# Pooled attention with a mixture-of-depths block on one core: two pairs of batches in block products, two key buffers, gate weights spread by TensorE, another order

## The chip, the cores and the metric

The kernel runs on one core of a Trainium2 chip. The core has five engines that work side by side, each through a queue of its own that it takes strictly in order: TensorE (PE, matrix products; the loading of its weights is shown as PEld), VectorE (DVE), ScalarE (ACT), GpSimd (POOL) and SyncE (SP, which here only issues transfers). The metric is the device time of one execution in microseconds (us), the median of several runs.

## What is computed

Eight batches (8 heads, 576 positions, head size 64) go through an attention whose keys and values are first averaged over eight neighbouring positions. The output, as rows of 512 numbers, goes through a mixture-of-depths block: in each batch the 128 rows with the highest gate score get a two-layer network added, the other rows stay as they are.

```python
k_p = k.reshape(B, H, Sp, pool, D).mean(axis=3)          # pool = 8
v_p = v.reshape(B, H, Sp, pool, D).mean(axis=3)
...
attn = attn / (np.sum(attn, axis=-1, keepdims=True) + 1e-09)
return np.matmul(attn, v_p).astype(np.float32)
...
scores = np.einsum('bsd,d->bs', x, w_gate)
out = x.copy()
for b in range(B):
    top_idx = np.argpartition(-scores[b], capacity)[:capacity]
    xe = x[b, top_idx]
    h = np.maximum(xe @ w1, 0.0)
    ye = h @ w2
    g = 1.0 / (1.0 + np.exp(-scores[b, top_idx]))
    out[b, top_idx] = x[b, top_idx] + g[:, None] * ye
```

The first layer is 512 by 1024, the second 1024 by 512.

## The kernel before

The work is cut into some 770 small steps, each with a name, an engine (or two or three engines that could do it), the buffers that it reads and writes, and a bank of PSUM. Three tables of numbers fix the program: `ORDER` lists all steps in one order, from which each engine takes its own steps as its queue; `HOMES` says which PSUM bank a group of products uses; `TURNS` says which of its engines a step runs on. Steps of different engines wait for each other only through the data.

For each batch b the steps are, with the names that the prediction uses:

- loads of keys, queries and values (k, q, v) from SP, 1 to 1.2 MB each. There is one key buffer `KR`, and two each of `QR` and `VR`.
- pooling of the keys and values in three halvings (kp, va on DVE or POOL; for batch 0 as products on PE), a product with the gate weights (vg, vt), copies (vd on ACT, then vl on POOL) that give the pooled values their last form; transposes of keys and queries (kh, kt, qt).
- scores on PE (s at line 635, sl at 652), exponentials on ACT (x, xl; lines 619 and 622), products with the values on PE (a at line 724, al at 736), reciprocals and scaling (r, z, n), and the store of the rows (o) from SP or ACT into the output.
- gate scores (sc), ranking by comparison of every row with every other (c where the row is spread by PE, cs where it goes through memory; line 825), a one-hot matrix (oh), its product with the position numbers on PE (pk, line 848), the reduction to an index (tk), and then on POOL the index (ix, line 858) with the gather of the 128 chosen rows from the output (line 859). PE turns the gathered rows (tu, line 879), DVE computes their gate (gd, line 866).
- the two layers: `dense(b)` has 8 products up (u, line 903; 8 records of the trace each) and 8 down (d, line 917). POOL scatters the result (pt, line 932).

Batches 6 and 7 are done together by `twin(6, 7)`: both layers as two-by-two block products in the manner of Strassen and Winograd, seven block products in place of eight (p1 to p7, line 999, 16 records each; q1 to q7, line 1063, 8 records each). For this the sums of weight blocks (wt, wr), of row blocks (sa) and of hidden blocks (sd) are formed by DVE and POOL at line 963 (`sum_`), and the products' outputs are put together by DVE (line 1012, `add_bank`) and ACT. The weight sums live in the buffers `QR` and `VR`, so they follow the last query and value. The list of products in one `twin` depends on DVE and ACT between them:

```python
        product(j7, 1.79, up(T[2][0], s3[0], j7, False), [T[2][1], s3[1]], p + 4, "p7")
        r, ws = claim(kr, m3[1])
        add_bank(m3[0], ws, j7, m1[0], [m1[1]] + r, p - 5000, "mb")
        product(j5, 1.79, up(T[0][0], s1[0], j5, False), [T[0][1], s1[1]], p + 5, "p5")
```

The transfers of SP and ACT share eight lanes, taken in turn; a transfer does not start before the one that held its lane eight transfers earlier has landed, and while it waits, the queue of its engine stands still.

Of the kernel before, what the change touches and what calls it, by code (L numbers as in the profile page):

```python
# [96 lines left out]
"""  # L97
TABLE = [[int(x) for x in t.split()] for t in (ORDER, HOMES, TURNS)]
ON_PE = (0,)
AGO = 500  # L100
BY_ROW = (4,5,6,7)
ON_CHIP = ()
PAIRED = ((6,7),)


class Plan:

# [1409 lines left out]
```

## Time and profile before

| | |
|---|---|
| median of the runs | 234.33 us (234.19 to 234.65) |
| the profiled execution | 235.51 us, of which the traced span is 233.7 us |
| PE busy | 210.5 us, 90% of the span |
| DVE, POOL, ACT busy | 152.3, 119.0 and 77.4 us |
| mean granted TensorE clock | 0.973 of full speed |
| bytes moved | 48.37 MB, a mean of 207 GB/s |

The span is the time between the first and the last event of the trace; 1.81 us of the profiled execution lie around it. PE is busy nearly all of the second half; its gaps lie in the first half, where the transfers are dense as well. The rows themselves stand in a section further down.

### The profile page before, as it was taken

Reading aid. Unit: us, or ns where it says so; the run is one execution under the profiler, and the core shown is the slowest. Engines: PE = TensorE matmul, PEld = TensorE weight load, DVE = VectorE, ACT = ScalarE, POOL = GpSimd, SP = SyncE. Lnnn points to the kernel's source line nnn. Section 1 sums busy time; section 2 is a strip of 40 time slices with the busy share of each in tenths; the row PEclk is TensorE's granted clock in tenths of the full one; section 3 lists DMA queues with packets and bytes.
Section 4 is the critical chain, followed back from the end, with each engine's and each line's share of the span. In section 5 each row is a group of like instructions: output and inputs, shape, how many; then the busy total and the mean of one; then the engine's idle time right before and its main releaser. Section 6 shows DMA issues by size and latency. Waiting matters only on the chain. (4 is left out here: it accounts for less than half of the span.)

```text
span 233.7 us, 6973 instructions
## 1 busy us (share of the span) xinstructions
PE 210.5 (90%) x2886; PEld 144.4 (62%) x2886; DVE 152.3 (65%) x362; ACT 77.4 (33%) x269; POOL 119.0 (51%) x155
## 2 busy tenths in 40 slices
PE   7869799757788999997899999999999999999990
PEld 3464444524535898743454799736488965986880
DVE  4268799944797996887429499973995511128460
ACT  2006356617563024524326243313460340010100
POOL 7016797968995499528031054144600556870531
PEclk9999999995899999999799999999999999999997
DMA  6999989999999489989921622434206441000112
GB/s 190 349 403 337 385 276 340 307 382 383 383 400 405 173 234 382 391 291 326 414 67 24 195 66 72 144 113 76 70 0 185 147 127 46 3 1 0 50 45 97
DMA packets 17815, 48.37 MB, mean 207 GB/s; under 512 B 2416, under 2 KB 2544, under 8 KB 15984
## 3 DMA queue, kind: packets, MB, share of 16 engines
q1 hardware_dynamic: 13552, 39.04, 46.8%
q10 hardware_dynamic: 2944, 4.62, 6.5%
q0 software_dynamic: 1280, 4.20, 5.5%
q8 instruction: 24, 0.39, 0.7%
q14 instruction: 15, 0.12, 0.2%
HBM read 36.31 MB, written 11.54 MB: 205 GB/s over the span
## 5 line engine op out<-in xcount | busy, mean ns | idle before, releaser
L903 PE MATMUL pJ<-xg,w 128*128 128x128 f32 x256 | 31.3, 279 | 0.0
L903 PEld LDWEIGHTS pJ<-xg,w 128*128 128x128 f32 x256 | 29.4, 192 | 2.9 <-issue 2.5
L932 POOL DMA_INDIRECT out_dram<-y,ix x8 | 8.9, 1118 | 42.0 <-DVE y L922 37.1
L917 PE MATMUL pA<-w,ht 128*128 128x512 f32 x48 | 24.0, 630 | 0.0
L619 ACT ACTIVATE em<-pG 128x1024 f32<-128x1024 f32 x16 | 16.4, 1028 | 22.3 <-PE pG L635 18.1
L917 PE MATMUL pJ<-w,ht 128*128 128x512 f32 x48 | 23.5, 606 | 0.0
L613 DVE STREAM_TRANSPOSE qt<-qr 128x1280 f32<-128x1280 f32 (+1 forms) x16 | 21.5, 1351 | 0.9 <-DMA qr<-in_q_dram 0.9
L635 PE MATMUL pG<-qt,kt 32*64 32x256 f32 (+1 forms) x512 | 19.6, 413 | 2.1 <-ACT em L619 1.2
L825 DVE SCALAR_TENSOR_TENSOR cmp<-row,sc,lar 128x576 bf16<-128x576 f32 (+1 forms) x20 | 17.5, 877 | 3.6 <-DMA row<-score_line 3.3
L682 POOL TENSOR_TENSOR vr<-vr 128x512 f32<-128x512 f32 (+1 forms) x12 | 19.4, 1618 | 0.0
L635 PEld LDWEIGHTS pG<-qt,kt 32*64 32x64 f32 x512 | 10.0, 133 | 12.1 <-ACT em L619 3.7
L585 POOL TENSOR_TENSOR kr<-kr 128x512 f32<-128x512 f32 (+1 forms) x8 | 11.3, 1410 | 11.4 <-DMA kr<-in_k_dram 11.4
L736 PE MATMUL pG<-vl,el 32*64 32x264 f32 x156 | 13.6, 425 | 3.4 <-POOL vl L707 2.8
L776 ACT ACTIVATE xs<-pG,rz 128x64 f32<-128x64 f32 (+1 forms) x64 | 14.0, 336 | 5.8 <-DVE rz L767 4.5
L724 PE MATMUL pG<-vs,em 64*64 64x66 f32 x624 | 14.7, 224 | 1.2 <-issue 0.9
L866 DVE SCALAR_TENSOR_TENSOR dots<-xr,wr 128x512 bf16<-128x512 f32 x8 | 8.7, 1083 | 10.7 <-DMA xr<-out_dram,ix 10.7
L724 PEld LDWEIGHTS pG<-vs,em 64*64 64x64 f32 x624 | 12.5, 135 | 4.4 <-issue 2.4
L858 POOL TENSOR_SCALAR ix<-tk 128x1 int32<-128x1 f32 x8 | 2.2, 273 | 25.4 <-DVE tk L854 22.5
L917 PEld LDWEIGHTS pA<-w,ht 128*128 128x128 f32 x48 | 8.8, 202 | 9.1 <-issue 9.1
L917 PEld LDWEIGHTS pJ<-w,ht 128*128 128x128 f32 x48 | 8.2, 190 | 7.4 <-issue 7.4
L859 POOL DMA_INDIRECT xr<-out_dram,ix x8 | 9.0, 1119 | 6.2 <-DMA out_dram<-xs 3.1
L903 PEld LDWEIGHTS pG<-xg,w 128*128 128x128 f32 x96 | 11.4, 192 | 1.0 <-issue 1.0
(210 smaller groups left out, 425.9 us busy)
## 6 DMA issues: line engine op xcount, KB each, us to landing
vr<-in_v_dram SPq DMA_DIRECT2D x8, 1024.0 KB, 8.0
kr<-in_k_dram SPq DMA_DIRECT2D x7, 1152.0 KB, 7.8
qr<-in_q_dram SPq DMA_DIRECT2D x7, 1152.0 KB, 6.4
out_dram<-xs SPq DMA_DIRECT2D x18, 256.0 KB, 8.2
w<-in_moe_w_dram SPq DMA_DIRECT2D x4, 1024.0 KB, 8.1
out_dram<-xs ACTq DMA_DIRECT2D x14, 256.0 KB, 4.9
vr<-in_v_dram SPq DMA_DIRECT2D x16, 64.0 KB
out_dram<-xs SPq DMA_DIRECT2D x7, 128.0 KB
```

Source lines behind the costliest of these rows:

```text
L585: e.tensor_tensor(out=x[:, a:z, 0:2], in0=x[:, a:z, 0:2], in1=x[:, a:z, 2:4], op=OP.add)
L613: nc.vector.transpose(out=QT[b % 2].rearrange("p j x t g -> p t (j x) g")[:, lo:hi], in_=QR[b % 2][:, lo:hi].rearrange("p t (x g) -> p t x ...
L619: note(nc.scalar.activation(to[:, :, 0:256].rearrange("p m (h x) -> p m h x", h=2), of[:, :, :, 0:16].rearrange("p m h t g -> p m h (t g)" ...
L635: note(nc.tensor.matmul(pG[64 * s : 64 * s + 64, r, 0:n], KT[i][rows, j, (SP - NL) * s + NL : (SP - NL) * s + SP], QT[i][rows, j, 2 * s : ...
L682: g.tensor_tensor(out=x[:, a:z, 0:4], in0=x[:, a:z, 0:4], in1=x[:, a:z, 4:8], op=OP.add)
L724: note(nc.tensor.matmul(acc[64 * z : 64 * z + 64, s, E * m : E * m + E], EM[h][i][64 * s : 64 * s + 64, m, AT[c] + 64 * z : AT[c] + 64 * z ...
L736: note(nc.tensor.matmul(pair(jobs[c])[64 * z : 64 * z + 64, s, 0 : NP * E], EL[i][x : x + 32, AT[c] + 64 * z : AT[c] + 64 * z + 64], VL[i] ...
L776: note(nc.scalar.activation(to[:, s, m], o[:, s, m, 0:D], AF.Copy, scale=rz[:, NP * s + m : NP * s + m + 1]))
L825: note(nc.vector.scalar_tensor_tensor(cmp[0:n], row()[0:n, 0:S], SC[i][0:n, c : c + 1], after_, op0=OP.subtract, op1=OP.is_ge, accum_out=R ...
L859: j = nc.gpsimd.indirect_dma_start(out=XR[x], out_offset=None, in_=out_rows[0 : (b + 1) * S], in_offset=bass.IndirectOffsetOnAxis(ap=IX[x] ...
L903: note(nc.tensor.matmul(single(ju)[:, cap * f : cap * f + cap], w1[g][:, d, 128 * f : 128 * f + 128], XG[i][:, d, :], start=(d == 0), stop ...
L917: note(nc.tensor.matmul(single(jd)[0:cap, :], HT[i][f // 4][:, f % 4, :], w2[f // 4][:, f % 4, :], start=(f == 0), stop=(f == FB - 1)))
```

## The change

- `PAIRED` holds two pairs: batches 4 and 5 are done by a `twin` as well, so four batches are left to `dense`. The weight sums are formed once, for the first pair.
- `KR` is two buffers, even and odd batches apart. The results of the second layer in `twin` (N tiles) sit in `KR[1]` and no longer behind the M tiles in the one buffer.
- The gate weights came as two broadcasts of 112 KB and one of 256 KB from memory. Now 2 KB are loaded, two products with a row of ones spread them on PE (gw0, gw1), and two copies store them (gc0, gc1).
- The gate score (sc) and the one-hot matrix (oh) may also run on POOL: sc of batches 0, 1 and 3 to 7, and oh of batches 2, 3 and 5 do. Other steps changed engine in the table too (DVE has 257 steps before and 261 now, POOL 83 and 99, ACT 120 and 131, SP 79 and 71, PE 231 and 215).
- Some helper tiles are in bf16; the test that the ranks are sound counts now the found rows (`found`) and not the sum of the ranks.
- All three tables are new.

```diff
 ORDER = """
-    0 2 16 4 763 12 11 759 25 23 17 18 760 5 14 24 15 6 26 3 20 38 22 21 27 7 33 13 40 28 89 30 99 29 41 31 39 42 43
+    2 16 15 4 18 17 0 20 768 3 6 11 12 769 26 7 19 27 92 28 767 23 5 29 30 31 102 101 25 32 771 41 42 24 14 43 36 13
...
-PAIRED = ((6,7),)
+SHARED = 0
+PAIRED = ((4, 5), (6, 7))
...
-    KR = sb("kr", [128, TG, D])
+    KR = sb("kr", [128, TG, D], n=2)
...
-            dma(KR, src, 128 * 256 * TG, p, (), [("KR", 0), ("KR", 1)], name=f"k{b}")
+            dma(KR[b % 2], src, 128 * 256 * TG, p, (), [("KR", b % 2, 0), ("KR", b % 2, 1)], name=f"k{b}")
...
-        for x in range(2):
-            dma(WG[64 * x : 64 * x + 64].rearrange("p m e -> p (m e)")[:, 0 : DM - D], bass.AP(tensor=t, offset=o + D * x, ap=[[0, 64], [1, DM - D]]),
-                64 * 1792, 2.4, (), [("WG", x)], rate=330e3, cost=0.5, free=True, name=f"g{x}")
+        add("POOL", 0.12, lambda: nc.gpsimd.memset(onerow, 1.0), (), ["onerow"], -90, name="onerow")
+        dma(WR[0:1], bass.AP(tensor=t, offset=o, ap=[[0, 1], [1, DM]]), 2048, -80, (), ["WR"], rate=2e3, cost=0.5, free=True, name="g0")
...
+        def wide():
+            note(nc.tensor.matmul(single(jb)[:, 0:DM], onerow, WR[0:1], start=True, stop=True))
...
-        dma(WR, bass.AP(tensor=t, offset=o, ap=[[0, 128], [1, DM]]), 128 * 2048, 150, (), ["WR"], rate=350e3, cost=0.5, free=True, name="w3")
...
-        def score():
-            nc.vector.tensor_tensor(out=SS[i], in0=ZA[:, b, :, :, 1], in1=RZ[i], op=OP.mult)
-            nc.vector.tensor_reduce(out=SC[i], in_=SS[i], axis=AX.X, op=OP.add)
...
+        def score(e):
+            engine(e).tensor_tensor(out=SS[i], in0=ZA[:, b, :, :, 1], in1=RZ[i], op=OP.mult)
+            if e == "DVE":
+                nc.vector.tensor_reduce(out=SC[i], in_=SS[i], axis=AX.X, op=OP.add)
+                return
+            for w in (4, 2):
+                nc.gpsimd.tensor_tensor(out=SS[i][:, :, 0:w], in0=SS[i][:, :, 0:w], in1=SS[i][:, :, w : 2 * w], op=OP.add)
+            nc.gpsimd.tensor_tensor(out=SC[i], in0=SS[i][:, :, 0], in1=SS[i][:, :, 1], op=OP.add)
...
-        both((("DVE", 1.1), ("ACT", 2.45)), True, one_hot, [("RK", b, c) for c in range(NC)] + ["slots", "ones"], [held, "apart"], p + 0.6, name=f"oh{b}")
+                    engine(e).tensor_scalar(OH[:, c, :], mine(c), RK[:, b, c], None, op0=OP.is_equal)
+        both((("DVE", 1.2), ("ACT", 2.7), ("POOL", 2.1)), True, one_hot, [("RK", b, c) for c in range(NC)] + ["slots", "ones"], ["OH", "apart"], p + 0.6, name=f"oh{b}")
...
-        m1, m3 = (part(KR, f"M{t}", kr, 512 * t, 512, 4) for t in range(2))
+        m1, m3 = (part(KR[0], f"M{t}", kr, 512 * t, 512, 4) for t in range(2))
...
-        n1, n3, v3q, v2q, v2p = (part(KR, f"N{t}", kr, 1024 + 256 * t, 256, 1) for t in range(5))
+        n1, n3, v3q, v2q, v2p = (part(KR[1], f"N{t}", ks, 256 * t, 256, 1) for t in range(5))
```

What the new tables do is seen in the queues. Three places follow; a name with a number is one buffer; the line numbers of these steps are 16 higher in the changed kernel (25 for the turning of gathered rows).

The first is ACT's queue where batch 0's ranking ends and the pooled values of batch 2 are copied (`vs0`, the step vd2), in the kernel before:

```order
L837 ACTIVATE apart_115<-slots_152,rk_112 128x128 x5
L838 ACTIVATE oh_114<-apart_115,ones_154 128x640
L760 ACTIVATE za_146<-pG_166,eps_147 128x8
L761 COPY za_146<-pG_166 128x8
L435 DMA out_0_dram<-xs03_95 16x8x512
L701 COPY vs0_87<-vs0_87 32x66 x2
L760 ACTIVATE za_146<-pA_167,eps_147 128x8
```

And the same place in the changed kernel:

```order
L436 DMA out_0_dram<-xs00_94 16x8x512
L436 DMA out_0_dram<-xs04_98 16x4x512
L776 ACTIVATE za_146<-pG_165,eps_147 128x8
L777 COPY za_146<-pG_165 128x8
L865 ACTIVATE apart_116<-slots_152,rk_113 128x128 x5
L866 ACTIVATE oh_115<-apart_116,ones_154 128x640
L717 COPY vs0_88<-vs0_88 32x66 x2
```

Before, the store of `xs03` (o03) stood right ahead of the copy; now two other stores (o00 and o04) stand ahead of it, with the one-hot matrix between.

The second is PE's queue up to the turning of batch 2's gathered rows (`xr2`, tu2, last row). Before, it ended so:

```order
L917 MATMUL pA_167<-w20_144,ht00_136 128x512
L724 MATMUL pJ_168<-vs1_88,em01_82 64x66 x16
L724 MATMUL pG_166<-vs1_88,em11_84 64x66 x16
L736 MATMUL pJ_168<-vl1_90,el1_86 64x264
L736 MATMUL pG_166<-vl1_90,el1_86 64x264
L736 MATMUL pJ_168<-vl1_90,el1_86 64x264
L736 MATMUL pG_166<-vl1_90,el1_86 64x264
L736 MATMUL pJ_168<-vl1_90,el1_86 64x264
L736 MATMUL pG_166<-vl1_90,el1_86 64x264
L736 MATMUL pJ_168<-vl1_90,el1_86 64x264
L736 MATMUL pG_166<-vl1_90,el1_86 64x264
L879 MATMUL pG_166<-ident_151,xr2_132 128x128 x4
```

In the changed kernel it ends so:

```order
L933 MATMUL pJ_167<-w20_144,ht00_136 128x512
L933 MATMUL pJ_167<-w21_145,ht01_137 128x512 x3
L740 MATMUL pG_165<-vs0_88,em00_82 64x66 x16
L740 MATMUL pG_165<-vs0_88,em10_84 64x66 x16
L752 MATMUL pG_165<-vl0_90,el0_86 64x264 x8
L933 MATMUL pJ_167<-w21_145,ht01_137 128x512
L933 MATMUL pJ_167<-w20_144,ht10_138 128x512 x2
L838 MATMUL pA_166<-ident_151,sc1_109 128x128 x4
L838 MATMUL pA_166<-ident_151,sc1_109 128x64
L904 MATMUL pG_165<-ident_151,xr2_132 128x128 x4
```

Between batch 2's pick (pk2) and this turning stood six d products, two blocks of scores, one block of value products and the spreading of a score row (sp). Now ten d products, the value products of more than a whole block (72 at line 740 and 18 at 752, of which the rows show 32 and 8) and an sp stand there.

The third is the end of PE's queue. Before, the last rows of the program were these (batches 6 and 7):

```order
L1063 MATMUL pA_167<-w20_144,ht00_136 128x256 x4
L1063 MATMUL pG_166<-vr0_70,qt1_80 128x256 x4
L1063 MATMUL pG_166<-vr1_71,qt1_80 128x256 x4
L1063 MATMUL pG_166<-vr0_70,qt1_80 128x256 x4
L1063 MATMUL pA_167<-w21_145,ht01_137 128x256 x4
L1063 MATMUL pG_166<-vr1_71,ht11_139 128x256 x4
L1063 MATMUL pG_166<-w21_145,qt1_80 128x256 x4
```

In the changed kernel they are these (line 1015 is the first layer of a pair, 1079 the second, 1142 the sum for the final test):

```order
L1079 MATMUL pA_166<-w21_145,qt1_81 128x256 x4
L1015 MATMUL pG_165<-qt0_80,qr0_69 128x128 x8
L1142 MATMUL pJ_167<-seen_159,ones_154 1x2
L1015 MATMUL pG_165<-xg1_135,qr1_70 128x128 x8
L1079 MATMUL pG_165<-w20_144,ht00_136 128x256 x4
L1015 MATMUL pG_165<-qt0_80,w11_143 128x128 x8
L1079 MATMUL pA_166<-vr1_72,qt1_81 128x256 x4
L1079 MATMUL pA_166<-vr0_71,qt1_81 128x256 x4
L1079 MATMUL pG_165<-vr0_71,qt1_81 128x256 x4
L1079 MATMUL pG_165<-w21_145,ht01_137 128x256 x4
L1079 MATMUL pG_165<-w21_145,qt1_81 128x256 x4
L1079 MATMUL pA_166<-vr1_72,ht11_139 128x256 x4
```

Before, products of `dense` batches stood among the pair's first-layer products (line 917 rows, not shown); now the second pair's products have only the end of the first pair's among them.

## Rows read from the trace of the kernel before

**Rows 1.** The page, part 1: busy time, share of the span, instructions.
```profile
PE 210.5 (90%) x2886; PEld 144.4 (62%) x2886; DVE 152.3 (65%) x362; ACT 77.4 (33%) x269; POOL 119.0 (51%) x155
```

**Rows 2.** Stretches: length, busy PE, PEld, DVE, ACT, POOL, granted clock, DMA share, GB/s.
```profile
0.00:75.34 75.34, 60.67 (x1123) 35.09 (x1123) 54.16 (x118) 33.43 (x114) 51.85 (x83) 0.95 0.97 349
53.70:60.50 6.80, 6.32 (x124) 4.10 (x132) 4.26 (x10) 3.69 (x19) 6.27 (x10) 0.50 1.03 374
75.34:227.75 152.41, 149.78 (x1767) 109.27 (x1763) 97.66 (x243) 44.01 (x155) 66.02 (x70) 0.99 0.43 141
99.20:109.74 10.54, 10.54 (x167) 5.14 (x166) 8.26 (x17) 3.18 (x7) 5.36 (x6) 1.00 0.89 303
111.70:115.20 3.50, 3.40 (x7) 1.91 (x8) 2.08 (x5) 1.36 (x2) 0.00 (x0) 0.51 1.08 435
180.00:228.00 48.00, 47.74 (x287) 38.02 (x285) 19.70 (x51) 6.87 (x16) 24.76 (x24) 1.00 0.16 51
```

**Rows 3.** The chain that ended last: start, time on the chain, what.
```profile
183.54 2.68 PE pJ L903 x24
186.22 3.44 PE pA L917 x8
...
198.54 5.36 PE pG L999 x48
...
217.38 5.18 PE pG L1063 x24
...
227.78 0.50 DVE y L1069
```

**Rows 4.** PE's waits: for what, us in total, times, the longest.
```profile
PE pG L736 <- POOL vl L707: 2.8, 1, 2.8
...
PE pG L879 <- DMA xr<-out_dram,ix: 2.1, 1, 2.1
...
PE pA L724 <- DVE cmp L825: 1.5, 1, 1.5
PE pJ L1109 <- DVE tk L854: 1.2, 1, 1.2
PE pG L635 <- ACT em L619: 1.2, 1, 1.2
...
PE pG L635 <- ACT za L761: 0.8, 1, 0.8
```

**Rows 5.** Timeline of ACT, 44 to 58 us: start, length, what, idle before.
```profile
47.46 0.16 ACT L761 COPY za<-pG 128x8 f32<-128x8 f32 x1
52.25 0.56 ACTq L435 DMA_DIRECT2D out_dram<-xs  x1
52.85 0.51 ACT L701 COPY vs<-vs 32x66 f32<-32x66 f32 x2 [5.23 <-DMA vr<-in_v_dram]
```

**Rows 6.** Timeline of SP's transfers, 41 to 47 us.
```profile
41.54 2.63 SPq L435 DMA_DIRECT2D vr<-in_v_dram  x2
```

**Rows 7.** Timeline of POOL, 47 to 56 us.
```profile
53.45 0.62 POOL L707 TENSOR_TENSOR vl<-vs,inside 128x264 f32<-128x264 f32 x1 [1.62 <-ACT vs L701]
```

**Rows 8.** Timeline of PE, 46 to 64 us: the first product after the stop.
```profile
54.12 0.69 PE L736 MATMUL pG<-vl,el 32*64 32x264 f32 x1 [2.80 <-POOL vl L707]
```

**Rows 9.** Timeline of PE, 98.8 to 116.5 us, around batch 2's gather.
```profile
99.13 0.28 PE L848 MATMUL pA<-aux,oh 128*128 128x2 bf16 x5
...
107.94 0.70 PE L724 MATMUL pJ<-vs,em 64*64 64x66 f32 x32
...
111.80 1.11 PE L879 MATMUL pG<-ident,xr 128*128 128x128 f32 x4 [2.06 <-DMA xr<-out_dram,ix]
```

**Rows 10.** Timeline of DVE, 158 to 168 us: the gate product of batch 4.
```profile
162.11 3.07 DVE L866 SCALAR_TENSOR_TENSOR dots<-xr,wr 128x512 bf16<-128x512 f32 x1
```

**Rows 11.** Timeline of POOL, the same stretch: a weight sum.
```profile
162.26 2.36 POOL L963 TENSOR_TENSOR qr<-w,w 128x1024 f32<-128x1024 f32 x1
```

**Rows 12.** The tile `dots`, all eight gate products: shortest, median, longest, ns.
```profile
L866 DVE SCALAR_TENSOR_TENSOR dots<-xr,wr x8: 674/692/3072, 70.7 to 214.2; 128x512 bf16<-128x512 f32 x8
```

More of the change, by code (lines that the diff above doesn't have):

```diff
@@ L340, in direct_path @@
     VL = sb("vl", [128, NP, E], n=2)
[L341 removed]
+    WG = sb("wg", [128, NP + 1, D])
+    onerow = sb("onerow", [1, 128])
     XS = [[sb(f"xs{i}{c}", [128, DM]) for c in range(NC)] for i in range(2)]
@@ L398, in single @@
         return pG[:, x] if x < 4 else (pA, pJ)[x // 2 - 2][:, x % 2]
-    beside = {}
+    beside, turns = {}, {}
     def note(ins, other=None):
@@ L478, in line @@
             nc.gpsimd.memset(RK, -1.0)
-        add("POOL", 3.1, line, (), ["slots"] + [(x, i, c) for x in ("SS", "RZ") for i in range(2) for c in range(NC)]
+        add("POOL", 3.3, line, (), ["slots"] + [(x, i, c) for x in ("SS", "RZ") for i in range(2) for c in range(NC)]
             + [("RK", b, c) for b in range(B) for c in range(NC)] + [("VR", i, 1) for i in range(2)], -89, name="line")
@@ L524, in small @@
             nc.gpsimd.memset(want[:, 0:1], float(128 * B * NC * H))
-            nc.gpsimd.memset(want[:, 1:2], float(B * (S * (S - 1) // 2 - 64)))
-        add("POOL", 0.6, small, (), ["ones", "want"] + [("Z", b, NC - 1) for b in range(B)], -60, name="small")
+            nc.gpsimd.memset(want[:, 1:2], float(B * cap))
+            nc.gpsimd.memset(seen, 0.0)
+        add("POOL", 0.6, small, (), ["ones", "want", "seen0", "seen1"] + [("Z", b, NC - 1) for b in range(B)], -60, name="small")
     def load_kq(b):
@@ L556, in load_gate, with halves @@
         t, o = moe_w_gate.tensor, moe_w_gate.offset
-        for x in range(2):
-            dma(WG[64 * x : 64 * x + 64].rearrange("p m e -> p (m e)")[:, 0 : DM - D], bass.AP(tensor=t, offset=o + D * x, ap=[[0, 64], [1, DM - D]]),
-                64 * 1792, 2.4, (), [("WG", x)], rate=330e3, cost=0.5, free=True, name=f"g{x}")
+        add("POOL", 0.12, lambda: nc.gpsimd.memset(onerow, 1.0), (), ["onerow"], -90, name="onerow")
+        dma(WR[0:1], bass.AP(tensor=t, offset=o, ap=[[0, 1], [1, DM]]), 2048, -80, (), ["WR"], rate=2e3, cost=0.5, free=True, name="g0")
+        ja, jb = plan.job(ONES), plan.job(ONES)
+        def halves():
+            for x in range(2):
+                note(nc.tensor.matmul(single(ja)[64 * x : 64 * x + 64, 0 : NP * D], onerow[:, 0:64],
+                                 WR[0:1].rearrange("p (m x d) -> p m x d", x=2, d=D)[:, :, x], start=True, stop=True))
+        def wide():
+            note(nc.tensor.matmul(single(jb)[:, 0:DM], onerow, WR[0:1], start=True, stop=True))
+        add("PE", 0.6, halves, ["onerow", "WR"], [], 10, job=ja, mode=12864, name="gw0")
+        add("PE", 0.86, wide, ["onerow", "WR"], [], 11, job=jb, name="gw1")
+        both((("DVE", 0.4), ("ACT", 0.4)), False, lambda e: copy(e, WG[:, 0:NP], single(ja)[:, 0 : NP * D].rearrange("p (m d) -> p m d", d=D)),
+             [], [("WG", 0)], 10, job=ja, name="gc0")
+        both((("DVE", 0.65), ("ACT", 0.62)), False, lambda e: copy(e, WR, single(jb)[:, 0:DM]), [], ["WR"], 11, job=jb, name="gc1")
         for x in range(2):
@@ L586, in go @@
                 e.tensor_tensor(out=KS[:, a:z], in0=x[:, a:z, 0], in1=x[:, a:z, 1], op=OP.add)
-            both((("DVE", (1.35, 1.15)[n]), ("POOL", (2.41, 2.14)[n])), b < 2, go, [("KR", n)], [("KR", n), ("KS", n)], 100 * b - 60 + n,
+            both((("DVE", (1.35, 1.15)[n]), ("POOL", (2.41, 2.14)[n])), b < 2, go, [("KR", b % 2, n)], [("KR", b % 2, n), ("KS", n)], 100 * b - 60 + n,
                  name=f"kp{b}{n}")
@@ L689, in gate @@
             engine(e).tensor_tensor(out=x[:, :, 2], in0=VS[i][:, :, 0:D], in1=WG[:, :, 0:D], op=OP.mult)
-        both((("DVE", 0.5), ("POOL", 0.88)), b < 1, gate, [("VS", i, 0), ("VS", i, 1), ("WG", 0), ("WG", 1), ("WGL", 0), ("WGL", 1)], [("VR", i, 0), ("VR", i, 1)], p, name=f"vg{b}")
+        both((("DVE", 0.5), ("POOL", 0.88)), b < 1, gate, [("VS", i, 0), ("VS", i, 1), ("WG", 0), ("WGL", 0), ("WGL", 1)], [("VR", i, 0), ("VR", i, 1)], p, name=f"vg{b}")
         def total():
@@ L794, in rank @@
         p = 100 * b + 20
-        def score():
-            nc.vector.tensor_tensor(out=SS[i], in0=ZA[:, b, :, :, 1], in1=RZ[i], op=OP.mult)
-            nc.vector.tensor_reduce(out=SC[i], in_=SS[i], axis=AX.X, op=OP.add)
-        add("DVE", 0.52, score, [("RZ", i, c) for c in range(NC)], [("SC", i)] + [("SS", i, c) for c in range(NC)], p - 70,
+        def score(e):
[6 more added lines that the diff above has]
+            nc.gpsimd.tensor_tensor(out=SC[i], in0=SS[i][:, :, 0], in1=SS[i][:, :, 1], op=OP.add)
+        both((("DVE", 0.7), ("POOL", 0.9)), True, score, [("RZ", i, c) for c in range(NC)], [("SC", i)] + [("SS", i, c) for c in range(NC)], p - 70,
             name=f"sc{b}")
@@ L821, in rank, with count, mine @@
             n = ROWS[c]
-            def count(c=c, n=n):
+            def count(e, c=c, n=n):
+                row_ = row()[0:n, 0:S]
+                to = (cmpa if c < SHARED else cmp)[0:n]
+                turns[b, c] = e
+                if e == "ACT":
+                    note(nc.scalar.activation(to, row_, AF.Sign, bias=SC[i][0:n, c : c + 1], scale=-1.0, accum_out=RK[0:n, b, c]))
+                    return
                 after_ = LAT[0:n, LAST - OFF[c] : LAST - OFF[c] + S] if jr is not None else LAR[0:n, NC - 1 - c : NC - 1 - c + S]
-                note(nc.vector.scalar_tensor_tensor(cmp[0:n], row()[0:n, 0:S], SC[i][0:n, c : c + 1], after_,
+                note(nc.vector.scalar_tensor_tensor(to, row_, SC[i][0:n, c : c + 1], after_,
                                                     op0=OP.subtract, op1=OP.is_ge, accum_out=RK[0:n, b, c]))
-            if jr is None:
-                add("DVE", 0.9, count, ["ROW", ("SC", i), "LAR"], [("RK", b, c), "cmp"], p + c * 0.1, name=f"cs{b}{c}")
-            else:
-                add("DVE", 0.87, count, [("SC", i), "LAT"], [("RK", b, c), "cmp"], p + c * 0.1, job=jr, name=f"c{b}{c}")
-        one, held = (OH, "OH") if b not in ON_CHIP else (apart, "apart")
+            alts = (("DVE", 0.88), ("ACT", 0.95))[: 1 + (c < SHARED)]
+            key = "cmpa" if c < SHARED else "cmp"
+            both(alts, True, count, (["ROW", "LAR"] if jr is None else ["LAT"]) + [("SC", i)], [("RK", b, c), key], p + c * 0.1,
+                 job=jr, name=f"cs{b}{c}" if jr is None else f"c{b}{c}")
+        def mine(c):
+            return slots if turns[b, c] == "DVE" else odd
         def one_hot(e):
@@ L862, in index @@
             gath[b] = [j]
[L863 removed]
+        add("POOL", 1.9, index, [("TK", b)] + [("ROWS", b, c) for c in range(NC)], [("IX", x), ("XR", x)], p - 90,
             late=2.4, mark=b, name=f"ix{b}")
[L866 to L867 removed]
+        add("DVE", 1.0, lambda: nc.vector.scalar_tensor_tensor(cmp[0:cap, 0:DM], XR[x], 1.0, WR[0:cap], op0=OP.mult, op1=OP.mult, accum_out=GV[x]),
+            [("XR", x), "WR"], [("GV", x), "cmp"], p, name=f"gd{b}")
         add("ACT", 0.25, lambda: nc.scalar.activation(GV[x], GV[x], AF.Exp, scale=-1.0), (), [("GV", x)], p, name=f"ge{b}")
@@ L949, in twin @@
         vr = [[("VR", i, h) for h in range(2)] for i in range(2)]
-        kr = [("KR", 0), ("KR", 1)]
+        kr, ks = ([("KR", i, n) for n in range(2)] for i in range(2))
         qt = [[("QT", i, h) for h in range(2)] for i in range(2)]
```

80 lines of the change are left out of this document (33 added, 47 removed), and 86 rows, old and new, of tables (HOMES, ORDER, TURNS).

## The prediction, made before the changed kernel had run

> **What bounds the kernel now.** I read the page's busy times first: PE works 90% of the span, no other engine over 65% [rows 1]. So the second view was the stretches. From the first product of `dense(0)` at 75.34 to the last product at 227.75 PE is busy 149.78 of 152.41 us; in the 75.34 us before that only 60.67, with the transfers at 0.97 of their time and 349 GB/s [rows 2]. PE is the bound behind 75, and what feeds it is the bound ahead of it. The third view was the granted clock: two stretches, 53.70 to 60.50 and 111.70 to 115.20, ran at 0.50 and 0.51 [rows 2], the lower level of 1.2 GHz; half their length, 3.4 and 1.7 us, is lost work even though PE counts as busy. Each stands behind a wait of PE: 2.80 us at 54.12 for the pooled values [rows 8] and 2.06 at 111.80 for gathered rows [rows 9]. The fourth view, PE's waits, names these two as the longest that a new order can move, and four smaller ones of 1.5, 1.2, 1.2 and 0.8 [rows 4]. Behind the last product only its blend of 0.50 at 227.78 [rows 3], a scatter and the end of the span remain; both kernels end so.
>
> The sum is made against the profiled execution's own 235.5; the median of the runs is 1.2 lower, and the forecast is given on the median.
>
> **The products.** By the chain, 24 records of u take 2.68 us and 8 of d 3.44 [rows 3]. A u has 8 records, so 0.893; a d has 2, so 0.86. Two dense batches are 16 of each: 14.3 + 13.8 = 28.05. Forty-eight records of p take 5.36 and 24 of q 5.18: 1.787 per p (16 records), 1.727 per q (8). Seven of each are 24.6. **-3.5**. The pair brings no weight sums of its own, but some two dozen more additions, copies and scalings on DVE, ACT and POOL. They lie beside PE: from 180 to 228 DVE was busy 19.70 of 48 us and POOL 24.76 [rows 2]. Where they don't, they are a cost of the handovers, below.
>
> **The stop at 50 to 60.** ACT finished a copy at 47.6 and then stood until 52.25, when the store o03 left; the copy vd2 behind it began at 52.85 [rows 5], vl at 53.45 [rows 7], PE's products at 54.12 [rows 8]. o03 waited for its lane, held by the values of batch 3 that SP issued at 41.54 [rows 6]. The new queue has o00 and o04 there. Their lanes are held by the last piece of batch 2's own values, for which vd2 needs to wait anyway, and by batch 3's queries, which SP issues two transfers later. So I take the whole stop as gone: 2.80 of wait and 3.4 of clock, **-6.2** (bounds 0 and -6.2). Late next are batch 0's comparisons and the one-hot on ACT, ahead of vd2 in the new queue.
>
> **The gather of batch 2.** Its pick began at 99.13 and its rows were there at 111.80, 12.7 us later; PE had 10.5 of work until 109.74 [rows 2, 9]. The new queue holds ten d (8.6) and the value products: 64 records at line 724 with 16 at 736 took 1.80 from 107.94 [rows 9] to 109.74, and 144 and 36 stand there now, 4.05. With 12.7 of work even without the sp, the wait is covered, if barely: 2.06 and 1.7 of clock, **-3.8** (bounds 0 and -3.8).
>
> **Early waits.** Batch 1's keys have a buffer of their own and stand third in SP's queue, and 0.48 MB of broadcasts (1.4 us at 349 GB/s) are gone from the saturated stretch. The four smaller waits sum to 4.7 [rows 4]. Some are ranking that only moves; I take half, **-2.3** (bounds 0 and -4.7). The products and copies that spread the gate weights run before the first keys have landed; without that cover they cost about 1, two copies of the size of the 0.69 of a gate product [rows 12].
>
> **What comes back.** Three things are new on PE's path. Batches 0 and 1 have their gathers earlier, where transfers are dense: one wait like that of batch 2 with its clock, 3.8. The second pair stands at the end without dense products between its block products, so each must find its sums ready. And 16 more steps run on POOL: while a weight sum of 2.36 ran there [rows 11], a gate product took 3.07 on DVE in place of the median's 0.69 [rows 10, 12], a loss of 2.4. I take one such meeting on the path: **+6.2** (bounds 0 and +12.4, both twice).
>
> The Trainium skill, page "SBUF — State Buffer", section "Who interferes with whom", says that a VectorE instruction with two SBUF inputs and a GpSimd instruction that reads SBUF exclude each other for the whole instruction, whichever began first. The trace agrees with it where 0.69 became 3.07 beside 2.36. The rule speaks against this change, which puts more on POOL: by it every meeting costs its whole length and not a share, so two meetings more on the path would make the sum 4.8 worse.
>
> **The sum**: 235.5 - 3.5 - 6.2 - 3.8 - 2.3 + 6.2 = 225.9, on the median 224.7; I say 225. The changes of type to bf16, the counted rows of the final test and the tiles that share a place move only steps that nothing waits for.
>
> **Rivals.** (a) *The losses come back in another place.* The transfers are at 0.97 of their time until 75 [rows 2], and a queue that no longer waits at 50 meets a lane, a load or a gather later. Then only the products' saving stays: 235.5 - 3.5 = 232.0, on the median 230.8. For it speaks that PE lost work in the front from many causes, against it that the new queues ask for batches 1 and 2 with fewer bytes ahead. Chance 0.20. (b) *The front's gain comes whole*, with no new wait: 225.9 - 6.2 = 219.7, on the median 218.5, or 216 with all the early waits gone. PE was busy 47.74 of 48 us in the last stretch [rows 2], so handovers can be hidden; but there dense products did the hiding. Chance 0.12. (c) *The second pair waits on POOL*: seven block products each held by a sum or a scaling that stands behind a POOL step of 2.4 us. It outweighs the gains of 15.8 from the seventh on: 7 x 2.4 = 16.8, so 236.5, on the median 235.3. DVE's and POOL's idle halves speak against seven in a row, the in-order queue of POOL with gathers and scatters between the sums speaks for it. Chance 0.10 of slower, and 0.05 that it just balances (within 0.2%, about what a measurement can tell from no change).
>
> **How the numbers follow.** The forecast's own case has 0.53, with a range of 220 to 229. The range for 8 in 10 takes in (a) at 230.8 with a margin and most of (b): 217.5 to 233. Below it lies the far end of (b), 0.04; above it the balance, (c) and a little of (a), 0.16. Faster 0.53 + 0.20 + 0.12 = 0.85, the same 0.05, slower 0.10.
>
> **What the changed kernel's profile would show.** Products: p at 1.79 and q at 1.73 per block product, four dense batches, 14 of each pair. Stop: no gap of PE over 2 us around batch 2's value products, no half clock there, and the copy vd2 begins within 1 us of its reduction. Gather: no wait of tu2. Early waits: the first product of `dense(0)` at 57 to 64 in place of 75.34 (less work stands ahead of it there). Handovers: the second pair's products without gaps over 1 us; more than three such gaps speak for (c). The forecast is wrong if the first dense product stands later than 68, which is (a) in the front, or if PE's waits behind 150 us sum to more than 6.

## The result, and the profile of the changed kernel

The changed kernel takes 226.68 us (median of four runs, 225.63 to 227.75) where the kernel before takes 234.49 beside it (four runs, 234.19 to 236.34): a ratio of 0.965, interval 0.958 to 0.973. The forecast was 225.0 with a range of 217.5 to 233. The profiled execution took 227.75, against 235.51 for that of before; the sums below go by the traces of these two. Some executions of a kernel take longer than its others at a lower granted clock; the ratios here leave those out, the medians and ranges do not.

The page's busy times (the line that answers to [rows 1]):

```profile
PE 209.0 (93%) x2900; PEld 149.1 (66%) x2900; DVE 162.2 (72%) x359; ACT 76.7 (34%) x273; POOL 138.1 (61%) x205
```

POOL is 19 us busier and DVE 10, PE 1.5 less. Where the time came from is seen in the stretches, with the columns of [rows 2]. The first product of `dense(0)` now begins at 64.26 and the last product of all ends at 219.64:

```profile
0.00:64.26 64.26, 54.10 (x946) 31.89 (x946) 44.72 (x101) 25.99 (x88) 44.43 (x86) 0.97 0.93 344
64.26:219.63 155.37, 153.17 (x1960) 116.79 (x1953) 116.99 (x258) 50.75 (x185) 92.52 (x118) 1.00 0.49 162
26.00:32.00 6.00, 4.85 (x128) 3.50 (x136) 2.98 (x5) 1.84 (x6) 5.77 (x7) 0.72 1.03 380
48.00:64.00 16.00, 13.70 (x338) 7.70 (x322) 12.32 (x26) 7.66 (x25) 14.46 (x21) 1.00 1.04 405
64.00:75.00 11.00, 9.48 (x234) 7.80 (x219) 8.05 (x23) 4.86 (x22) 3.83 (x5) 1.00 0.91 326
110.00:170.00 60.00, 59.32 (x924) 39.49 (x924) 48.53 (x112) 23.07 (x90) 38.91 (x53) 1.00 0.45 127
170.00:219.63 49.63, 49.63 (x347) 46.43 (x346) 33.95 (x75) 4.79 (x11) 20.76 (x20) 1.00 0.16 47
```

The front is 11.1 us shorter, the rest 3.0 longer: 8.1 in all (the executions differ by 7.8, as 0.4 more lies around this stretch in the changed kernel). These two are not yet gains, for work moved between them. Before, these rows stood ahead of `dense(0)` (PE's timeline of the kernel before; the scores of batch 4 at lines 635 and 652, the last value products of batch 3 at 724 and 736):

```profile
66.15 1.34 PE L635 MATMUL pG<-qt,kt 32*64 32x320 f32 x32
68.86 1.28 PE L652 MATMUL pJ<-qt,kl 128*32 128x320 f32 x16
70.08 1.12 PE L635 MATMUL pG<-qt,kt 32*64 32x256 f32 x32
71.13 0.69 PE L724 MATMUL pA<-vs,em 64*64 64x66 f32 x16
71.74 0.66 PE L736 MATMUL pA<-vl,el 32*64 32x264 f32 x4
72.38 1.17 PE L724 MATMUL pG<-vs,em 64*64 64x66 f32 x64
```

With the last 16 of line 736 (0.62 where nothing interrupts them) they are 6.5 us from start to start, waits and the turning between them left out, and in the changed kernel they stand behind the first product of `dense(0)`. So the front gained 11.1 - 6.5 = **4.6**. Behind it the time should have changed by +6.5 for these, -3.5 for the products and -3.8 for the gather, -0.8 in all; it changed by +3.0. **3.8** came back there. The split is good to about 1 us: in the second profile of the changed kernel, which ran again below, `dense(0)` begins at 65.11 and the execution took 227.43.

PE's waits in the whole span, with the columns of [rows 4]:

```profile
PE pG L571 <- POOL rz L476: 2.2, 1, 2.2
PE pG L651 <- DVE kt L616: 1.9, 1, 1.9
PE pG L740 <- issue: 1.8, 3, 0.9
PE pG L651 <- issue: 0.8, 1, 0.8
```

The first is the start, the second stands at 27.15 with half the clock behind it (the stretch 26 to 32 above, at 0.72), and 1.5 of the 1.8 lie at 67.44 and 73.10. No wait is listed behind 142.5. The large stops of [rows 8] and [rows 9] have no answer in this list.

The forecast's signs, one by one. The pooled values of batch 2 on ACT (timeline: start, length, what, idle before), whose reduction on DVE ran from 47.02 for 0.49:

```profile
47.54 0.50 ACT L717 COPY vs<-vs 32x66 f32<-32x66 f32 x2 [0.83 <-DVE vs L709]
```

The copy follows at once, and the batch's value products run behind it with no wait over 0.6 and at full clock (the stretch 48 to 64 above). The turning of batch 2's rows on PE has no wait either:

```profile
108.03 0.66 PE L904 MATMUL pG<-ident,xr 128*128 128x128 f32 x4
```

The chain at the end, with the columns of [rows 3], gives 1.79 per p, 1.73 per q, and the same end as before, a blend of 0.50:

```profile
176.18 1.79 PE pG L1015 x16
...
212.72 5.18 PE pG L1079 x24
217.90 1.74 PE pA L1079 x8
219.67 0.50 DVE y L1085
```

Both pairs run without a gap: 49.63 of 49.63 us busy in the last stretch, though POOL works 20.76 of it. Only the mark for `dense(0)`, 57 to 64, was missed, by 0.26.

### The profile page after: what moved, and what is told of

It is laid out like the page before. It is cut to its first block, busy times and chain, and to the rows that moved or that the text cites. A ratio compares the mean times of both kernels' runs of the same rounds, so it can differ in the third digit from the quotient of the medians.

```text
span 225.8 us, 7085 instructions
## 1 busy us (share of the span) xinstructions
PE 209.0 (93%) x2900; PEld 149.1 (66%) x2900; DVE 162.2 (72%) x359; ACT 76.7 (34%) x273; POOL 138.1 (61%) x205
## 4 chain that ended last, share of the span: by engine, by line
PE 75%; DMA 11%; DVE 7%; issue 3%; POOL 1%; POOLq 0%; ACTq 0%; SPq 0%; ACT 0%; DVEq 0%
PE pJ L919 7%; PE pJ L933 6%; PE pG L1015 6%; PE pG L933 6%; PE pG L1079 6%; PE pG L651 6%; DMA w<-in_moe_w_dram 5%; PE pA L1079 5%; PE pG L740 4%; DMA qr<-in_q_dram 3%; PE pG L752 3%; PE pA L919 3%; DMA vr<-in_v_dram 2%; PE pJ L1015 2%; PE pA L1015 2%
## 5 line engine op out<-in xcount | busy, mean ns | idle before, releaser
L919 PEld LDWEIGHTS pJ<-xg,w 128*128 128x128 f32 x160 | 18.8, 191 | 3.5 <-issue 3.0
L919 PE MATMUL pJ<-xg,w 128*128 128x128 f32 x160 | 20.8, 281 | 0.0
L610 DVE STREAM_TRANSPOSE kh<-ks 128x576 f32<-128x576 f32 x8 | 9.8, 1229 | 7.8 <-ACT ks L448 6.2
L933 PE MATMUL pJ<-w,ht 128*128 128x512 f32 x32 | 15.4, 608 | 0.0
L792 ACT ACTIVATE xs<-pG,rz 128x64 f32<-128x64 f32 x64 | 13.9, 343 | 4.1 <-DVE rz L783 4.0
L933 PE MATMUL pG<-w,ht 128*128 128x512 f32 x32 | 14.8, 599 | 0.0
L852 DVE SCALAR_TENSOR_TENSOR cmp<-pA,sc,lat 128x576 bf16<-128x576 f32 (+1 forms) x15 | 12.2, 812 | 0.5
L776 ACT ACTIVATE za<-pG,eps 128x8 f32<-128x8 f32 (+1 forms) x15 | 3.9, 272 | 24.6 <-PE pG L752 16.0
L792 ACT ACTIVATE xs<-pA,rz 128x64 f32<-128x64 f32 (+1 forms) x48 | 10.5, 327 | 4.4 <-DVE rz L783 2.8
L616 POOL TENSOR_TENSOR kt<-kh 128x288 f32<-128x288 f32 x6 | 4.9, 825 | 11.2 <-DVE kh L610 11.1
```

The costliest lines, as they stand in the source:

```text
L792: note(nc.scalar.activation(to[:, s, m], o[:, s, m, 0:D], AF.Copy, scale=rz[:, NP * s + m : NP * s + m + 1]))
L852: note(nc.vector.scalar_tensor_tensor(to, row_, SC[i][0:n, c : c + 1], after_, op0=OP.subtract, op1=OP.is_ge, accum_out=RK[0:n, b, c]))
L919: note(nc.tensor.matmul(single(ju)[:, cap * f : cap * f + cap], w1[g][:, d, 128 * f : 128 * f + 128], XG[i][:, d, :], start=(d == 0), stop ...
L933: note(nc.tensor.matmul(single(jd)[0:cap, :], HT[i][f // 4][:, f % 4, :], w2[f // 4][:, f % 4, :], start=(f == 0), stop=(f == FB - 1)))
```

## The experiments

Each ratio is against the kernel before on the same chip. That kernel's median was 235.32 us beside the runs on the products and on the later store, with and without the gather's edit; 232.88 beside the earlier store, with and without it, the later gate products and the two warming products; and 233.24 beside the other four.

**The products: dense layers for batches 4 and 5.**

```diff
-PAIRED = ((4, 5), (6, 7))
+PAIRED = ((6, 7),)
```

The 32 dense products stand where the pair's block products stood; everything ahead stays. The changed kernel ran again beside it.

> The changed kernel with batches 4 and 5 done by dense products again (PAIRED is ((6, 7),)), all other steps in the changed kernel's order, the 32 dense products standing where the pair's 14 block products stood. My theory (7 x (1.787 + 1.727) against 16 x (0.893 + 0.86), nothing of it lost at the handovers): 3.5 us slower than the changed kernel, about 230.2 us. Rival (the second pair's handovers cost part of it, and dense products between the block products give it back): less than 1.5 us slower, under 228.2 us.

> The changed kernel itself, unchanged, on the same chip as the three others, so that they have something to stand against: 225.6 to 227.8 us. If the half clock at 28 to 31 us of its profile is there in some executions and not in others, single times fall into two groups near 225.8 and 227.6 us; if it isn't that, they spread evenly.

Measured: 232.76 us, ratio 0.988 (0.984 to 0.992); the changed kernel again 227.54, ratio 0.964 (0.958 to 0.971). The difference of 5.2 is more than the term. From the first product behind `dense(3)` to the last of all the two profiles differ by 55.36 - 50.81 = 4.55 us, and of this one wait is the replacement's own, where the one pair that is left follows the dense blend (PE's timeline):

```profile
206.55 2.05 PE L1015 MATMUL pG<-qt,qr 128*128 128x128 f32 x16 [0.84 <-DVE y L938]
```

4.55 - 0.84 = 3.7: the product term of 3.5 holds.

The eight executions of the changed kernel (four in the result, four here) do fall into two groups. Three with a mean granted clock of 0.998 to 1.000 took 225.63 to 225.94 us, five with 0.989 to 0.992 took 227.41 to 228.23. So the half clock comes in some executions and hardly in others, and about 1.8 us go with it. The two profiled ones, 227.75 and 227.43, are of the longer group.

**The stop at 50 to 60, first form: the store later.** In the kernel before, o03 goes from ahead of vd2 to behind the next rows' scaling.

```diff
 ACT of the kernel before
-L435 DMA out_dram<-xs_95 16x8x512
 L701 COPY vs_87<-vs_87 32x66 x2
 ...
 L776 ACTIVATE xs_92<-pG,rz_104 128x64 x8
+L435 DMA out_dram<-xs_95 16x8x512
```

> The kernel before with one change: in ACT's queue the store o03 stands eight steps later, behind the scaling n20 and no longer ahead of the copy vd2. Nothing else moves. My theory (the store's wait for its lane held vd2, so PE stopped 2.8 us and ran 3.4 us of work at half clock): 6.2 us faster than before, about 228.3 us, and no stretch of half clock between 50 and 62 us. Rival (the front is bound by its transfers, so the wait shows up again a few microseconds later): within 2 us of the kernel before, 232.5 to 234.5 us.

Measured: 239.14 us, ratio 1.015 (1.006 to 1.024), slower. The wait of 2.80 is gone, but others stand behind it, and the clock is at 0.51 from 59 to 65 (PE's timeline of this run):

```profile
59.10 2.00 PE L635 MATMUL pG<-qt,kt 32*64 32x256 f32 x27 [1.71 <-issue]
62.25 2.44 PE L635 MATMUL pG<-qt,kt 32*64 32x320 f32 x32 [1.15 <-ACT em L619]
...
71.12 0.63 PE L879 MATMUL pJ<-ident,xr 128*128 128x128 f32 x4 [2.58 <-DMA xr<-out_dram,ix]
```

The last is new: batch 0's gather reads the rows that o03 stores. On POOL it left at 64.42 after 5.42 us of waiting for a store; before, it left at 60.13 after 0.29:

```profile
64.42 1.21 POOL L859 DMA_INDIRECT xr<-out_dram,ix  x1 [5.42 <-DMA out_dram<-xs]
```

So this form moves a second thing, and does not price the stop alone.

**The same with the gather of batch 2 given more cover.**

```diff
 PE of the kernel before
-L879 MATMUL pG<-ident,xr_132 128x128 x4
 L917 MATMUL pA<-w_144,ht_136 128x512
 L917 MATMUL pA<-w_145,ht_139 128x512 x3
+L879 MATMUL pG<-ident,xr_132 128x128 x4
```

> The kernel before with the store o03 moved as in the run before, and with the turning of batch 2's gathered rows (tu2, with its copy xg2) four d products later in PE's queue. My theory: another 3.8 us (2.06 of wait and 1.7 of clock), 10.0 in all, about 224.5 us, and neither of the two stretches of half clock is left. Rival (PE waits later for the same gather, or for what hangs on it): no more than 1.5 us gained on the run before, 227 us or more.

Measured: 237.29 us, ratio 1.008 (1.005 to 1.012). By the ratios it is 1.5 us less than the run before it (1.9 by the medians), and the two intervals overlap. In fact the edit had no wait to remove. In the run before it, where the turning stands in its old place, PE does not wait there (PE's timeline of that run; with the edit the turning stands at 116.46, without a wait too):

```profile
113.20 0.66 PE L879 MATMUL pG<-ident,xr 128*128 128x128 f32 x4
```

The work of PE from pick to turning is the same 10.5 us there as in the kernel before. What differs is how long the gather took (POOL's timeline, the kernel before and then the run with the later store):

```profile
102.85 1.05 POOL L859 DMA_INDIRECT xr<-out_dram,ix  x1 [0.59 <-DMA out_dram<-xs]
106.38 1.05 POOL L859 DMA_INDIRECT xr<-out_dram,ix  x1 [0.59 <-DMA out_dram<-xs]
```

From there to the turning it was 8.95 us in the kernel before, with a wait, and 6.82 in the run with the later store, without one. So the wait of [rows 9] came of a gather that took longer in the one execution that was profiled, why is open, and the edit prices nothing of it.

**The stop, second form: the store earlier.** To leave batch 0's gather alone, o03 goes up ACT's queue.

```diff
 ACT of the kernel before
 L622 ACTIVATE em_83<-pG 128x4x4x8 x2
+L435 DMA out_dram<-xs_95 16x8x512
 L435 DMA wr<-in_moe_w_gate_dram 128x512
 ...
-L435 DMA out_dram<-xs_95 16x8x512
 L701 COPY vs_87<-vs_87 32x66 x2
```

> The kernel before with one move: the store o03 (its rows are ready long before) leaves ACT ten transfers earlier, ahead of the keys of batch 4, in place of right ahead of the copy vd2. Unlike the run that moved it later, batch 0's gather waits for nothing new here. Theory A (the stop at 54 is worth its whole term): the wait of 2.80 at 54.12 and the half clock behind it are gone, vd2 starts within 1 us of its reduction, the first product of dense(0) comes 4 to 6 us before 75.34, and the time falls by 4 to 6.2 us, a ratio of 0.974 to 0.983. Rival B (the front is bound by the transfers and the loss comes back in another wait before 75): the wait at 54 is gone or smaller, but dense(0) begins within 2 us of 75.34 and the ratio is 0.992 to 1.01.

> The same, and with it the turning of batch 2's gathered rows (tu2) behind the product d16. Theory A (both terms whole): 6.2 and 3.8 less than before, about 224.5 to 227 where before has 234.5, a ratio of 0.957 to 0.968. Rival B (each comes back in part): 1.5 to 3 us less than the run with the store alone, as the same move gave 1.9 beside the other placing of the store, and a ratio of 0.98 to 1.0.

Measured: with the store alone 230.95 us, ratio 0.991 (0.986 to 0.995); with the gather's edit as well 230.82, ratio 0.993 (0.990 to 0.997). The stop is worth 232.88 x 0.0093 = 2.2 us (1.1 to 3.2 by the interval), not 6.2, and the gather's edit nothing beside it. ACT, in the second's trace:

```profile
49.14 0.52 ACT L701 COPY vs<-vs 32x66 f32<-32x66 f32 x2 [1.06 <-DVE vs L693]
```

The copy starts 3.7 us earlier than in [rows 5]. On PE the stop is broken up, not gone, and half clock follows all the same (timeline, then the stretch):

```profile
57.69 1.11 PE L635 MATMUL pG<-qt,kt 32*64 32x256 f32 x27 [1.13 <-issue]
60.03 2.27 PE L635 MATMUL pG<-qt,kt 32*64 32x320 f32 x32 [1.24 <-ACT em L619]
...
73.31 2.05 PE L903 MATMUL pJ<-xg,w 128*128 128x128 f32 x16
```

```profile
60.00:64.00 4.00, 3.97 (x45) 2.07 (x49) 3.97 (x6) 3.18 (x11) 3.84 (x5) 0.57 1.01 347
```

`dense(0)` begins 2.0 us earlier than in [rows 2]. Behind it this profile is 3.7 shorter than that of before, nearly the whole gather term. But the gather's edit is not the reason: in the run with the store alone that part is 3.5 shorter, and its turning, in the old place, does not wait either:

```profile
111.11 0.66 PE L879 MATMUL pG<-ident,xr 128*128 128x128 f32 x4
```

So of three profiles with the turning in its old place one has the wait. The two without it are 1.5 us (later store) and 3.5 us (earlier store) shorter behind the first product of `dense(0)`.

**One key buffer.** In the changed kernel all keys go to one buffer, and the loads of the keys of batches 1 and 2 stand later in SP's queue, as one buffer needs (that of batch 6 keeps its place there).

```diff
-dma(KR[b % 2], src, ...)
+dma(KR[0], src, ...)
```

> The changed kernel with all keys in one buffer again (the second one holds the N tiles alone), and with the key loads where one buffer lets them stand: batch 1's behind batch 0's queries as before the change, batch 2's behind batch 1's values, batch 6's behind the pooling of batch 5. Theory A (the second key buffer brings the early loads, and with them the front's gain): 3 to 6 us slower than the changed kernel, 230 to 233 us, and the first product of dense(0) 3 us or more later than 64.3. Theory B (the gain of the front lies in the order of the steps, not in the buffer): less than 1.5 us slower, under 229 us.

Measured: 234.19 us, ratio 1.005 (1.001 to 1.009): the whole gain of the change is gone. But little of it ahead of `dense(0)`, which begins at 65.8. SP's queue shows the place (timeline; the load of batch 5's keys is the second row):

```profile
54.85 0.70 SPq L436 DMA_DIRECT2D vr<-in_v_dram  x1
72.99 0.34 SPq L436 DMA_DIRECT2D kr<-in_k_dram  x1
```

These keys wait until the pooling on DVE has read batch 4's keys out of the buffer, and with them every transfer behind. In the changed kernel they leave at 53.83. There SP's queue stops as well, until 72.32 and for the same pooling, but at batch 6's keys: the rest of batch 4's values and batch 5's queries have left before the stop. The stretches behind, of this run:

```profile
66.00:75.00 9.00, 9.00 (x222) 7.81 (x223) 7.38 (x22) 4.94 (x22) 2.82 (x4) 1.00 0.23 54
75.00:113.00 38.00, 35.48 (x460) 22.89 (x460) 24.76 (x47) 16.70 (x59) 27.85 (x40) 0.96 0.98 369
```

and of the changed kernel:

```profile
66.00:75.00 9.00, 7.48 (x205) 6.06 (x205) 6.12 (x18) 3.35 (x19) 2.17 (x3) 1.00 0.89 311
75.00:113.00 38.00, 38.00 (x517) 24.27 (x516) 29.60 (x58) 19.19 (x67) 32.20 (x44) 1.00 0.93 328
```

The transfers stand at 0.23 of their time from 66 to 75; PE pays for it between 75 and 113, with 2.5 us of waits and 0.04 x 38 = 1.5 of clock. The second buffer is worth 5 to 8 us in this order: 5.2 between the two profiled executions (232.99 and 227.75), 7.6 between this median and those of two variants of the changed kernel on the same chip (226.62 and 226.63, below). The changed kernel itself did not run there. It is a price of this order with the loads moved, not of the best order for one buffer; and with the 5.2 us of the products it comes to more than the whole gain, so the two prices cannot be added.

**Gate weights by broadcast,** as before, in place of the two products and copies.

```diff
-dma(WR[0:1], bass.AP(tensor=t, offset=o, ap=[[0, 1], [1, DM]]), 2048, ...)
-add("PE", 0.6, halves, ...); add("PE", 0.86, wide, ...)
+dma(WR, bass.AP(tensor=t, offset=o, ap=[[0, 128], [1, DM]]), 128 * 2048, ...)
+two loads of 64 x 1792 bytes into WG
```

> The changed kernel with the gate weights broadcast by transfers as before (112 KB twice at the start, 256 KB at batch 2), without the two products, the two copies and the row of ones. Theory A (0.48 MB less in a saturated stretch is worth its transfer time): 1.4 us slower than the changed kernel, about 228.5 us. Theory B (the spreading products with the fillers behind them hold TensorE until 8.8 us while batch 0's keys have landed at 6.1, and cost as much as they save): no slower, 225.5 to 227.5 us, and the pooling of batch 0's keys begins before 7 us.

Measured: 226.62 us, ratio 0.969 (0.962 to 0.975): no change. PE pools the keys 3.6 us earlier, and then waits for values:

```profile
5.13 2.32 PE L578 MATMUL pJ<-kr,ident 128*128 128x320 f32 x8
...
14.52 3.08 PE L675 MATMUL pJ<-vr,ident 128*128 128x128 f32 x16 [3.15 <-DMA vr<-in_v_dram]
```

**The gate products later.** The two products go behind the pooling of batch 0's keys, their copies behind key steps of batch 1.

```diff
 PE of the changed kernel
-L571 MATMUL pG<-wr,onerow 128x512
-L567 MATMUL pJ<-wr,onerow 64x256 x2
 ...
 L590 MATMUL pG<-kr_67,ident 128x256 x4
+L571 MATMUL pG<-wr,onerow 128x512
+L567 MATMUL pJ<-wr,onerow 64x256 x2
```

> The changed kernel with the two gate products behind the pooling of batch 0's keys, and the two copies of them behind key steps of batch 1 on DVE. Theory A (the gate products delay the start by what the pooling of keys starts later, 8.77 against 5.17): pooling begins at 5 to 7, the first scores at 17.5 to 18.7 in place of 19.7, and the time falls by 1.0 to 1.6 us, a ratio to before of 0.957 to 0.962. Rival B (the start is bound by the values of batch 0 and what is won there is lost again before dense(0)): first scores at 19 or later or dense(0) still at 64.3, and no change within 0.7 us: 0.964 to 0.969.

Measured: 226.94 us, ratio 0.975 (0.969 to 0.982). Pooling starts at 5.89, but a warming product then waits for the copy (PE's timeline), and the first scores come at 20.53, later than in the changed kernel:

```profile
5.89 2.54 PE L590 MATMUL pJ<-kr,ident 128*128 128x320 f32 x8
...
13.71 2.07 PE L1125 MATMUL pJ<-ident 128*128 128x512 f32 x2 [0.88 <-DVE wg L450]
...
20.53 1.33 PE L651 MATMUL pG<-qt,kt 32*64 32x320 f32 x32
```

The early pooling did not bring the scores forward. The changed kernel did not run on that chip, so whether the higher ratio is this edit's or the chip's is open; there is no gain.

**Half clock at 28 to 31 filled.** One warming product (a matrix product whose result nobody uses) from the program's end goes ahead of batch 1's scores, where PE waits at 27.15; the last run does it with two, on top of the edit above.

```diff
 PE of the changed kernel
 L752 MATMUL pA<-vl_90,el_86 64x264 x2
+L1125 MATMUL pJ<-ident 128x512
 L651 MATMUL pG<-qt_81,kt_77 64x320 x16
```

> The changed kernel with one of the two filler products at the very end (busy7, 1.05 us, its result is read by nothing) moved ahead of batch 1's first scores, where PE waited 1.9 us and then ran at half clock from 28 to 31 us. Theory (the clock falls because PE stood idle there, and the executions near 225.8 are those in which it did not fall): the half clock at 28 to 31 us is gone, and the executions lie near 225.8 us, with a median 1 to 1.7 us under the changed kernel's. Rival (the clock falls for another reason, or the wait sets the time and not the clock): no change in the median, 226.7 to 227.5 us.

> The same as the run with late gate products, and two warming products on PE stand ahead of the scores s11 of batch 1, where the changed kernel waits 1.9 us at 27.15 with half clock behind it: one that stood ahead of batch 0's values and one from the program's end. Theory A (clock and wait of the front add up to time): first scores at 17 to 18, no half clock at 28 to 31, dense(0) 1.5 to 3 us before 64.3 and a ratio of 0.950 to 0.960. Rival B (as in the run with one filler, where the half clock moved to 56 to 67 us): dense(0) within 1 us of 64.3 and a ratio of 0.962 to 0.970.

Measured: with one product 226.63 us, ratio 0.968 (0.961 to 0.975); with two and the late gate products 228.20, ratio 0.982 (0.976 to 0.987). Neither is faster than the changed kernel. The first one's stretches:

```profile
24.00:32.00 8.00, 6.64 (x178) 3.66 (x166) 6.28 (x11) 4.23 (x10) 7.54 (x10) 1.00 1.04 388
56.00:67.00 11.00, 9.14 (x175) 5.54 (x174) 7.76 (x20) 4.01 (x14) 8.73 (x9) 0.84 1.04 402
```

The clock is whole at 24 to 32, and lost at 56 to 67 in its place: 0.16 x 11 = 1.8 us. With transfers at 1.04 of their time in both stretches, what was won at 28 was lost again before `dense(0)`, which begins at 66.48 here. As some executions of the changed kernel have hardly any half clock without an edit, one profile does not show that the product was the reason.

**POOL's new steps back on DVE:** all gate scores and the one-hot matrices of batches 2, 3 and 5.

```diff
 queues of the changed kernel, for each of these batches
-POOL: L813 TENSOR_TENSOR ss, L818 x2, L819 TENSOR_TENSOR sc
-POOL: L869 TENSOR_SCALAR oh<-slots,rk 128x128 x5
+DVE: L813 TENSOR_TENSOR ss, L815 TENSOR_REDUCE sc
+DVE: L869 TENSOR_SCALAR oh<-slots,rk 128x128 x5
```

> The changed kernel with the gate scores (sc, seven batches) and the one-hot matrices (oh, batches 2, 3 and 5) on DVE and no longer on POOL, at the same places of the order. Theory A (what runs on POOL holds up DVE's steps with two inputs, so the move to POOL cost part of the gain): 0.5 to 2.4 us faster than the changed kernel. Theory B (DVE is the engine that PE waits for in the front, and each step taken from it counts): 1 to 4 us slower, 228 to 231 us. If neither matters, within 0.5 us.

Measured: 227.59 to 237.5 us over five runs, median 234.46, too wide for a ratio. The fastest is no faster than the changed kernel's median, the others are well above it. In its profile, of an execution of 234.46, PE is busy 56.36 of the 60 us from 110 to 170, against 59.32, with one large stand:

```profile
121.64 0.69 PE L752 MATMUL pG<-vl,el 32*64 32x264 f32 x12 [2.79 <-issue]
```

What the stand has to do with the edit is not shown. There is no sign that the steps cost more on POOL than on DVE; the run is inconclusive on how much they save.

## Why the prediction was right, and which of its terms were not

- **The products, -3.5:** right. 3.7 by the traces of the experiment, 5.2 by its medians with the handover and the rest of that order.
- **The stop, -6.2, and the early waits, -2.3:** both mis-sized. Together the front gained 4.6 of the 8.5. The step that failed is "so I take the whole stop as gone": the store was the cause of that wait, and in the changed queue it is gone as foretold, but the 3.4 of half clock and the 2.80 of wait were not its price: with the store moved, PE could not keep what it had won. Where the store alone was moved up, 2.2 remained, as PE met the next unfinished piece at 57.69 and 60.03. The front runs at the rate of the transfers (0.93 of their time, 344 GB/s in the changed kernel), so a wait that is removed there is mostly put off. That is rival (a), and in the front it came true by half.
- **The gather, -3.8:** the wait and its half clock are gone, as the row at 108.03 shows. But the step "the wait is covered" is not shown: the turning waited for nothing in two runs that left it in its old place (113.20 and 111.11), and moving it gained nothing beyond the noise. The forecast took one slow gather of one execution for a property of the order. In the sums here the term counts because the profiled execution of before had that wait; how often others have it is open.
- **What comes back, +6.2:** the size behind `dense(0)` was 3.8, if the gather counts with its 3.8, and the mechanism was another. No gather waits behind 64.26 and no handover of the pairs does. Of the 3.8, 1.5 is PE's idle time at 64 to 75, two stands ahead of value products that nothing in the profile explains. They go with an early `dense(0)`. Where it begins at 63.99 (the run with dense layers for batches 4 and 5) PE stands 2.14 us from 66 to 75, at 64.26 it stands 1.52, at 65.11 (the changed kernel again) 0.70, and in the four with the late start (one key buffer, the broadcast, the later gate products, one warming product; 65.83 to 67.30) nothing. Only the run with two warming products, at 67.11, has one of 0.46 again. The rows of the first and the third:

```profile
66.00:75.00 9.00, 6.86 (x200) 5.54 (x200) 6.05 (x16) 2.72 (x16) 1.97 (x3) 1.00 0.94 333
66.00:75.00 9.00, 8.30 (x213) 6.86 (x212) 6.38 (x19) 4.11 (x22) 2.24 (x4) 1.00 0.87 313
```

So this part reads as the front's own gain, put off once more; what holds these products is not shown. Of the rest, first-layer products lost 1.4 more than before: nine of their seventeen pieces are single products, which take 0.98 to 1.09 to the next step where one in a long piece takes 0.893. One block of value products took 1.70 from 140.61 to 142.31 where the fast ones take 0.52, 0.39 of it a wait.
- **The lock term in it, 2.4:** not met. The eight gate products of the changed kernel (shortest, median, longest, ns):

```profile
L891 DVE SCALAR_TENSOR_TENSOR cmp<-xr,wr x8: 649/683/1209, 61.3 to 200.7; 128x512 bf16<-128x512 f32 x8
```

The longest took 1.21 where before one took 3.07 [rows 12], beside a POOL step of 0.73 that began at 61.20. Another step of DVE took longer still, a comparison of batch 4's ranking, whose like take 0.82 (DVE's timeline):

```profile
128.06 2.92 DVE L852 SCALAR_TENSOR_TENSOR cmp<-row,sc,lar 128x576 bf16<-128x576 f32 x1
```

Beside it POOL worked on keys and pooled values. PE did not wait for it. The Trainium skill, page "SBUF — State Buffer", section "Who interferes with whom", has DVE and POOL exclude each other for a whole instruction; the row of the gate products agrees with it in kind. Its price on the path here was nil.
- **The gate weights, "about 1 if the cover is gone":** the cover was gone. The warming products and gate products keep PE until 8.77, where pooling began at 5.17 before, and the first scores came at 19.70 in place of 18.13. But neither the broadcast nor the later products made the kernel faster, so nothing of it reaches the end.
- **The rivals:** (c) did not appear. (b) failed in the front and was right on the handovers.

The sum on the profiled basis: -4.6 - 3.5 - 3.8 + 3.8 = -8.1, where -9.6 was forecast. The front fell short by 3.9, the return by 2.4; the errors partly cancel, so that the number was better than its parts is luck. That the gain does not survive without the second key buffer and the loads that it allows was not a term at all: the forecast costed the buffer under the early waits, and the run shows that it matters through SP's queue, later than I looked.
